# Keys and values of a head pair as two halves of 64 rows, products in two quadrants, zero products in waits, g_norm scaled late

## The chip, the cores and the metric

The kernel runs on one core of a Trainium2 chip. A core has five engines that run side by side and meet through semaphores: TensorE (matrix products; PE in the profile, with its weight loads as PEld), VectorE (DVE), ScalarE (ACT), GpSimd (POOL) and SyncE (SP), which here only issues DMAs. The metric is the device time of one launch in microseconds, the median of several runs; lower is better.

## The reference

Eight batches, eight heads, 576 tokens, head width 64. First a linear attention with a normalisation per head and token, then a block that mixes over tokens with waves of learned phases.

```python
kv  = einsum('bhsd,bhse->bhde', k, v)
out = einsum('bhsd,bhde->bhse', q, kv)
x   = out / sqrt(mean(out * out, -1) + 1e-6) * g_norm      # heads side by side: (8, 576, 512)
theta = x @ w_theta
y = w_tok_r @ (x * cos(theta)) + w_tok_i @ (x * sin(theta))
u = x + y
result = u + max(u @ w_ch, 0)                              # (8, 576, 512) float32
```

All inputs are float32; k^T v is computed in float32, the later products in float16 with float32 sums.

## The kernel before

**How the work is cut.** 576 tokens are four full tiles of 128 and a tail of 64 (`NF` = 4, `NT` = 5, `T` = 64). Heads are taken in pairs (`HP` = 4). For a batch:

- `load` (L274) issues the DMAs of q, k and v of a head pair. In batches 1 to 7 the tile is [128 rows, 2 heads, 4 tokens, 64], 256 KB in pieces of 1 KB, and the last 64 tokens of all heads come in extra loads `ql`, `kl`, `vl` (L301, 128 KB in pieces of 256 bytes); `kl` and `vl` land in the two constant buffers `tails`, whose rows 64 to 127 are zeroed once (L247). In batch 0 k and v come as [96 rows, 2 heads, 6 tokens, 64] (L282) and have no tails.
- `attention` (L483) forms k^T v of a head pair in float32 into PSUM: head 0 of the pair into partitions 0 to 63, head 1 into 64 to 127. That is ten products (five tiles by two heads, L498) in batches 1 to 7, twelve in batch 0 (six by two, L491), each in two records of the profile. `keep` (L510, L622) copies the result into a block diagonal float16 matrix `kvbd`, of which there are two, zeroed at the start.
- `cast_q`, `turn_q` turn q into float16 and transpose it (by DMA, L444, from batch 2 on; on TensorE in batches 0 and 1).
- `norm` (L524) for each tile: `raw` = q kv (L537), squares on ScalarE (L544), sums on VectorE (L548), the power -1/2 on GpSimd (L555, L559), x = raw times that (L571). Batch 0 has its own form in `first` (L593), by head pair, with roots on ScalarE.
- `turn_x` (L731): x transposed on TensorE and scaled by g_norm as it is copied out (L748; L680, L682 in batch 0). The scale `gcol` is loaded at the very start by two GpSimd DMAs (L943) and multiplied by 8 by a VectorE instruction (L376).
- `phase` (L760): theta (L770, L775), the whole turns taken off (L782, L786), sine and cosine (L805, L813), z = x times these (L823).
- `mix` (L845): eight results `y` of nine products each (L857) from z of all tiles and the transposed mixers `wT`; `uT` = y times gcol plus x^T (L865).
- `channel` (L878): u @ w_ch (L901), u transposed back (L892), the result (L912) and its store (L919, L924).

**Weights.** `load_weights` (L321) brings w_theta, the two token mixers and w_ch in chunks into staging buffers `wst` (four of them), and casts each on whichever of ScalarE, VectorE and GpSimd (L341, L343, L347) is chosen. `mixer_step` (L386) transposes the mixers on TensorE (L399) and copies them out (L407, L409).

**What sets the order.** Nothing runs as it is written down. Every piece is a task with its engines, planned costs, a due time, what it needs and which buffers it makes and uses. `Weave.run` (L74) walks through planned time: on each engine, among the tasks that could start within `SLACK` of the earliest, it takes the one with the earliest due time (`DUE`, by stage, batch and index), emits it, and notes planned ends. Loads keep one order of their own on SP; a load is put off while the planned DMA backlog is over `BACKLOG`. `in_traced_order` (L153) then pins each engine to the order in which the tasks were emitted. So each engine executes a fixed list, strictly in order, and waits where the plan was too hopeful. Planned costs never enter the program; they only shape these lists. How many buffers a kind of tile has is in `SLOTS`.

Of the kernel before, what the change touches and what calls it, by code (L numbers as in the profile page):

```python
# [21 lines left out]
    "load": (-17, 2.87),  # L22
    "first": (-0.52, 0.92),
    "cast": (-2.46, 2.3),
    "turn_q": (4.95, 0.2),
    "attention": (0.5, 3.82),
    "norm": (12.64, 4.8),
    "turn": (16.5, 4.83),
    "phase": (20.19, 4.95),
    "mix": (45.0, 2.9),  # L30
    "channel": (62.0, 4.75),
# [3 lines left out]
    "k": 5, "v": 5, "q": 6, "ql": 1, "tails": 2, "qc": 2, "qT": 2, "bd": 2, "sq": 2, "ss": 6,  # L35
    "rt": 6, "x": 9, "xT": 3, "pt": 2, "f": 2, "fa": 2, "tr": 2, "uT": 2, "u": 3, "ot": 3,
    "wst": 4, "z0": 2, "z1": 2, "z2": 2, "z3": 2, "z4": 2,
# [4 lines left out]
class Weave:  # L42
# [8 lines left out]
    SLACK = {"PE": 0, "ACT": 0.08, "DVE": 0.123, "POOL": 0.1, "SP": 0.05}  # L51
    MARGIN = {"PE": 0.014, "ACT": 0.018, "DVE": 0.106, "POOL": 0.1, "SP": 0.0}
    RATE = 0.335e6
    BACKLOG = 3.0
# [19 lines left out]
    def run(self):  # L74
        done, free, last = {}, {e: 0.0 for e in self.SLACK}, {}
# [22 lines left out]
        while ready:  # L98
            best = {}
            for t in ready:  # L100
                (name, engines, due, fn, needs, makes, uses, dma) = t
                if any(not self.slots[tag] for (tag, _) in makes):
                    continue
                at = max([done[n] for n in needs], default=0.0)
                for (tag, _) in makes:
                    at = max(at, min(self.slots[tag]))
                if dma is not None:
                    at = max(at, dma_free - self.BACKLOG)
                for (e, cost, lat) in engines:
                    start = max(free[e], at + self.MARGIN[e])  # L110
                    best.setdefault(e, []).append((start, due, at, t, cost, lat))
            picks = []
            for (e, c) in best.items():
                first = min(x[0] for x in c) + self.SLACK[e]
                (start, due, at, t, cost, lat) = min(
                    (x for x in c if x[0] <= first), key=lambda x: (x[1], x[0])
                )
                other = min(
                    (max(free[o], at) + k for (o, k, _) in t[1] if o != e), default=1e9
                )  # L120
                if other < max(free[e], at) + cost - 0.05:
                    start = max(start, other)
                picks.append((start, due, e, at, t, cost, lat))
            assert picks, [t[0] for t in ready][:40]
            (_, _, e, at, t, cost, lat) = min(picks, key=lambda x: x[:3])
            (name, engines, due, fn, needs, makes, uses, dma) = t
            start = max(free[e], at)
            free[e] = start + cost
            end = start + lat
            if dma is not None:  # L130
                (first, size, packed) = dma
                begin = max(start + first, dma_free)
                dma_free = begin + size / self.RATE / packed
                end = dma_free + 0.35
            done[name] = end
            for (tag, tile_name) in makes:
                pool = self.slots[tag]
                pool.remove(min(pool))
                last[tile_name] = 0.0
            fn(e)  # L140
            for tile_name in [n for (_, n) in makes] + list(uses):
                self.users[tile_name] -= 1
                last[tile_name] = max(last[tile_name], end)
                if self.users[tile_name] == 0:
                    self.slots[self.tag[tile_name]].append(last[tile_name] + 0.05)
            ready.remove(t)
            met(("t", name))
            for (_, tile_name) in makes:
                met(("b", tile_name))
        assert not wanted, list(wanted.items())[:5]  # L150
# [19 lines left out]
def kernel(  # L170
# [33 lines left out]
    NS = 6  # L204
    PS0 = S // NS
# [36 lines left out]
    tails = []  # L242
    for i in range(2):
        kl = const.tile([P, H, D], FP32, tag=f"kl{i}", name=f"kl{i}")
        vl = const.tile([P, H, D], FP32, tag=f"vl{i}", name=f"vl{i}")
        for t in (kl, vl):
            nc.gpsimd.memset(t[T:P], 0.0)  # L247
        tails.append((kl, vl))
# [21 lines left out]
    def dma(size, packed=1.0, first=1.4):  # L270
        return (first, size, packed)


    def load(b, hp):  # L274
# [3 lines left out]
        def part(kind, src):  # L278
            def fn(e):
                if b == 0 and kind != "q":  # L280
                    t = sb(kind, [PS0, 2, NS, D], FP32, f"{kind}{b}_{hp}")
                    nc.sync.dma_start(  # L282
                        out=t[:].rearrange("p h j d -> p h (j d)"),
                        in_=src[b, pair].rearrange("h (p j) d -> p h (j d)", j=NS),
                    )
                else:
# [4 lines left out]
                    )  # L291
                st[kind, b, hp] = t
            return fn

        def tail(kind, src):
            def fn(e):
                if kind == "ql":
                    t = sb("ql", [T, H, D], FP32, f"ql{b}")
                else:
                    t = tails[b % 2][0 if kind == "kl" else 1]  # L300
                nc.sync.dma_start(  # L301
                    out=t[0:T], in_=src[b, :, SF:S, :].rearrange("h s d -> s h d")
                )
                st[kind, b] = t
            return fn

        for (i, (kind, src)) in enumerate((("q", q), ("k", k), ("v", v))):
            weave.add((kind, b, hp), [SP], due("load", b, hp) + 0.01 * i, part(kind, src),
                      makes=[(kind, f"{kind}{b}_{hp}")], dma=dma(whole, 0.95), load=True)
        if hp == (0 if b else HP - 1):  # L310
            for (i, (kind, src)) in enumerate((("kl", k), ("vl", v), ("ql", q))):
                if b == 0 and kind != "ql":
                    continue
                weave.add((kind, b), [SP], due("load", b, hp) + (0.04 if b else -0.04) + 0.01 * i,
                          tail(kind, src),
                          makes=[("ql", f"ql{b}")] if kind == "ql" else
                          [("tails", f"tails{b}")] if kind == "kl" else [],
                          uses=[f"tails{b}"] if kind == "vl" else [],
                          dma=dma(whole / 2, 0.5), load=True)

    def load_weights():  # L321
# [13 lines left out]
        def cast(name, of, out, src, at, scale=1.0):  # L335
# [15 lines left out]
            weave.add(name, on, at, fn, needs=[of], uses=[of])  # L351

        at = due("load", 0, HP - 1) + 1.0
        for kc in range(NK):
            chunk(("wst", kc), moe_w_theta[kc * P:(kc + 1) * P, :], at + 0.01 * kc)
            cast(("wth", kc), ("wst", kc), wth[:, kc, :],
                 lambda kc=kc: st["wst", kc][:, 0:C], due("phase", 0, 0) - 1.0, FOLD)
        use = due("mix", 0, 0) - 8.0
# [10 lines left out]
        for kc in range(NK):  # L369
# [3 lines left out]
                 lambda kc=kc: st["wcs", kc][:, 0:C], due("channel", 0, 0) - 5.0)  # L373
# [5 lines left out]
        weave.add("gcol", [dve(0.1)], due("turn", 0, 0) - 2.0, gain)  # L379
# [3 lines left out]
        weave.add("sin", [("ACT", 1.5, 1.6)], due("phase", 0, 0), table,  # L383
                  needs=[("rt0", hp) for hp in range(HP + 1)])

    def mixer_step(n):  # L386
# [24 lines left out]
        at = due("mix", 0, 0) - 6.0 + 0.1 * n  # L411
# [71 lines left out]
    def attention(b, hp):  # L483
        def fn(e):
# [3 lines left out]
            if b == 0:  # L488
                for j in range(NS):
                    for r in range(2):  # L490
                        nc.tensor.matmul(  # L491
                            kvp[r * D:(r + 1) * D, hp, :], st["k", 0, hp][:, r, j, :],
                            st["v", 0, hp][:, r, j, :], start=(j == 0), stop=(j == NS - 1),
                        )
                return
            for j in range(NT):
                for r in range(2):
                    nc.tensor.matmul(  # L498
                        kvp[r * D:(r + 1) * D, hp, :],
                        st["k", b, hp][:, r, j, :] if j < NF else st["kl", b][:, 2 * hp + r, :],  # L500
                        st["v", b, hp][:, r, j, :] if j < NF else st["vl", b][:, 2 * hp + r, :],
                        start=(j == 0), stop=(j == NT - 1),
                    )

        def keep(e):
            for r in range(2):
# [4 lines left out]
                else:  # L511
                    nc.vector.tensor_copy(dst, src)

        weave.add(("kv", b, hp), [pe(0.84)], due("attention" if b else "first", b, hp), fn,
                  needs=[("k", b, hp), ("v", b, hp)] + ([("kl", b), ("vl", b)] if b else []),
                  makes=[] if hp else [("kv", f"kv{b}")],
                  uses=[f"k{b}_{hp}", f"v{b}_{hp}"] + ([f"tails{b}"] if b else [])
                  + ([f"kv{b}"] if hp else []))
# [419 lines left out]
    def due(stage, b, i):  # L938
        (first, every) = DUE[stage]
        return START + PERIOD * b + first + every * i  # L940

    for r in range(P // D):
        nc.gpsimd.dma_start(out=gcol[r * D:(r + 1) * D, :], in_=g_norm.unsqueeze(1))  # L943
    load_weights()
    for m in range(NM):
# [55 lines left out]
```

## Time and profile before

| | us |
|---|---|
| median of 5 runs | 244.79 (244.45 to 245.6) |
| the profiled execution | 243.88 |
| its span, first to last instruction | 242.1 |
| busy in the span: TensorE | 210.7 (87%), 2213 products |
| VectorE | 184.8 (76%) |
| ScalarE | 160.2 (66%) |
| GpSimd | 84.0 (35%) |
| DMA packets, share of 16 engines | 71.0% |
| products k^T v: L498 and L491 | 19.7 + 8.3 and 6.2 |

The span is what the trace covers; the time of a run is a little longer. Busy time of TensorE is the union of its records, whose ends are modelled, so a busy TensorE may still have room between its records; where times of single products are given below, they are distances from start to start. Rows of the profile name the line of the kernel, the engine, the tile written and the tiles read. A wait is put down to the instruction whose end released the waiting one.

### The profile page before, as it was taken

The page shows a single profiled execution, that of the slowest core. Times are in us where ns is not written, and L with a number is a line of the kernel's source. Part 1 is how long each engine was busy: PE and PEld are TensorE (multiplying, and loading weights), DVE is VectorE, ACT ScalarE, POOL GpSimd, SP SyncE. Part 2 cuts the span into 40 slices and gives each one's busy share as a digit, 9 for nine tenths or more (in the row PEclk, how much of TensorE's full clock was granted, in tenths as well). Part 3 has the DMA queues.
Part 4 walks back from the last instruction along what each step waited for, and adds up shares of the span by engine and source line. Part 5 has one row for each costly group of instructions (what it writes and reads, how often), then busy time and mean ns, then how long its engine had stood idle before and what let it go on. Part 6 is the DMA issues. An engine that isn't in the chain of part 4 may idle for free.

```text
span 242.1 us, 5707 instructions
## 1 busy us (share of the span) xinstructions
PE 210.7 (87%) x2213; PEld 144.7 (60%) x2213; DVE 184.8 (76%) x376; ACT 160.2 (66%) x303; POOL 84.0 (35%) x95
## 2 busy tenths in 40 slices
PE   0078586999997899989998999999999999999993
PEld 0066344777754675666665766766676766755861
DVE  1027669458996899789987997889879989998552
ACT  2036869763899288858884777677766797888021
POOL 7000034006550664076306640644136516640000
PEclk9999999599999999999999999999999999999999
DMA  6995589999946994995379986996499612002314
GB/s 186 219 204 152 154 273 232 329 355 232 341 94 165 316 250 95 274 368 126 77 188 265 331 100 172 279 317 170 100 259 337 94 63 109 26 22 87 111 43 152
DMA packets 60442, 46.41 MB, mean 192 GB/s; under 512 B 29056, under 2 KB 54144, under 8 KB 60416
## 3 DMA queue, kind: packets, MB, share of 16 engines
q1 hardware_dynamic: 60352, 46.05, 71.0%
q8 instruction: 17, 0.28, 0.5%
q14 instruction: 9, 0.07, 0.1%
q0 software_dynamic: 64, 0.00, 0.0%
HBM read 33.06 MB, written 9.44 MB: 176 GB/s over the span
## 4 chain that ended last, share of the span: by engine, by line
PE 32%; DVE 25%; POOL 21%; ACT 8%; DMA 8%; issue 4%; SPq 0%; DVEq 0%; POOLq 0%; ACTq 0%
POOL rt L559 16%; PE y L857 11%; DVE x L571 6%; DVE ss L548 5%; PE vps L901 4%; DMA gcol<-in_g_norm_dram 3%; PE kv L498 3%; POOL ss L555 3%; PE th L770 3%; DVE ot L912 3%; DVE f L786 3%; ACT tr L813 3%; DMA ql<-in_q_dram 3%; PE kv L491 2%; DVE z L823 2%
## 5 line engine op out<-in xcount | busy, mean ns | idle before, releaser
L857 PE MATMUL y<-wT,z 128*128 128x320 f16 (+1 forms) x576 | 79.1, 286 | 2.8 <-DVE z L823 1.4
L857 PEld LDWEIGHTS <-z 128*128 128x128 f16 x576 | 54.4, 98 | 19.5 <-issue 2.6
L559 POOL TENSOR_TENSOR rt<-ss,mhalf 128x8 f32<-128x8 f32 x35 | 61.8, 1765 | 2.9
L555 POOL TENSOR_SCALAR ss<-ss 128x8 f32<-128x8 f32 x35 | 11.9, 341 | 99.8 <-DVE ss L548 99.2
L748 ACT ACTIVATE xT<-xTps,gcol 128x512 f16<-128x512 f16 (+1 forms) x36 | 22.9, 637 | 22.2 <-PE xTps L739 22.2
L901 PE MATMUL vps<-wch,uT 128*128 128x512 f16 (+1 forms) x192 | 37.5, 344 | 0.0
L865 DVE SCALAR_TENSOR_TENSOR uT<-y,gcol,xT 128x256 f16<-128x256 f32 (+1 forms) x64 | 32.6, 511 | 6.4 <-PE y L857 6.2
L770 PE MATMUL th<-wth,xT 128*128 128x512 f16 x128 | 33.6, 390 | 0.2
L782 ACT ACTIVATE pt<-th,magic_t 128x512 f32<-128x512 f32 (+1 forms) x40 | 25.7, 642 | 11.8 <-PE th L770 9.2
L571 DVE TENSOR_TENSOR x<-raw,rt 128x512 f16<-128x512 f32 x36 | 24.8, 689 | 7.3 <-POOL rt L559 6.6
L908 ACT COPY u<-ups 128x512 f16<-128x512 f16 (+1 forms) x40 | 20.8, 538 | 12.6 <-PE ups L892 12.5
L912 DVE SCALAR_TENSOR_TENSOR ot<-vps,u 128x512 f32<-128x512 f32 (+1 forms) x40 | 25.0, 632 | 5.2 <-ACT u L908 3.2
L823 DVE TENSOR_TENSOR z<-x,tr 128x1024 f16<-128x1024 f16 (+1 forms) x40 | 25.7, 641 | 4.0 <-ACT tr L813 3.3
L548 DVE TENSOR_REDUCE ss<-sq 128x8 f32<-128x512 f32 x36 | 24.2, 679 | 2.7 <-ACT sq L544 2.5
L786 DVE SCALAR_TENSOR_TENSOR f<-pt,th 128x512 f32<-128x512 f32 (+1 forms) x40 | 25.1, 628 | 1.4 <-ACT pt L782 1.3
L805 ACT ACTIVATE tr<-f 128x512 f16<-128x512 f32 x32 | 20.2, 631 | 5.7 <-DVE f L786 5.3
L805 ACT ACTIVATE tr<-fa,pio_t 128x512 f16<-128x512 f32 x32 | 23.0, 718 | 1.0 <-DVE fa L793 1.0
L544 ACT ACTIVATE sq<-raw 128x512 f32<-128x512 f32 x36 | 20.9, 588 | 1.0 <-PE raw L537 0.9
L901 PEld LDWEIGHTS <-uT 128*128 128x128 f16 (+1 forms) x192 | 14.4, 102 | 9.2 <-issue 0.8
L498 PE MATMUL kv<-v,k 128*64 128x64 f32 x448 | 19.7, 234 | 0.0
L770 PEld LDWEIGHTS <-xT 128*128 128x128 f16 x128 | 11.9, 101 | 11.5 <-issue 1.5
L498 PEld LDWEIGHTS kv<-v,k 128*64 128x64 f32 x448 | 16.2, 143 | 4.2 <-issue 2.8
(83 smaller groups left out, 231.6 us busy)
## 6 DMA issues: line engine op xcount, KB each, us to landing
q<-in_q_dram SPq DMA_DIRECT2D x32, 256.0 KB, 5.7
out_dram<-ot SPq DMA_DIRECT2D x32, 256.0 KB, 5.0
k<-in_k_dram SPq DMA_DIRECT2D x28, 256.0 KB, 5.5
v<-in_v_dram SPq DMA_DIRECT2D x28, 256.0 KB, 5.7
k<-in_k_dram SPq DMA_DIRECT2D x4, 288.0 KB, 8.3
v<-in_v_dram SPq DMA_DIRECT2D x4, 288.0 KB, 9.4
wmix<-in_moe_w_tok_r_dram SPq DMA_DIRECT2D x4, 288.0 KB, 2.9
wmix<-in_moe_w_tok_i_dram SPq DMA_DIRECT2D x4, 288.0 KB, 3.5
```

The costliest lines, as they stand in the source:

```text
L498: nc.tensor.matmul(kvp[r * D:(r + 1) * D, hp, :], st["k", b, hp][:, r, j, :] if j < NF else st["kl", b][:, 2 * hp + r, :], st["v", b, hp][ ...
L548: nc.vector.reduce_sum(out=t[:], in_=st[sq][:].rearrange("p (h e) -> p h e", h=H), axis=mybir.AxisListType.X,)
L559: nc.gpsimd.tensor_tensor(out=r[:], in0=t[:], in1=mhalf[:], op=ALU.pow)
L571: nc.vector.tensor_tensor(out=t[:].rearrange("p (h e) -> p h e", h=H), in0=st[raw][:].rearrange("p (h e) -> p h e", h=H), in1=st[rt][:].un ...
L770: nc.tensor.matmul(t[:], xT[:, kc, :], wth[:, kc, :], start=(kc == 0), stop=(kc == NK - 1),)
L786: nc.vector.scalar_tensor_tensor(out=t[:], in0=st[pt][:], scalar=MAGIC, in1=st[th][:], op0=ALU.subtract, op1=ALU.subtract,)
L805: nc.scalar.activation(out=t[:, which, :], in_=src[:], func=AFT.Sin, scale=-RAD, bias=0.0 if bias is None else bias[:],)
L823: nc.vector.tensor_tensor(out=t[:], in0=xb.unsqueeze(1).broadcast_to((P, w, C)), in1=st[tr][:, 0:w, :], op=ALU.mult,)
L857: nc.tensor.matmul(t[:], z[:, kc * P:(kc + 1) * P], wT[m][:, cols], start=(m == 0), stop=(m == NM - 1),)
L865: nc.vector.scalar_tensor_tensor(out=st["uT", b][:, kc, cols], in0=st[y][:], scalar=gcol[:], in1=st["xT", b][:, kc, cols], op0=ALU.mult, o ...
L901: nc.tensor.matmul(t[half], uT(kc), wch[:, kc, r * n:(r + 1) * n], start=(kc == 0), stop=(kc == NK - 1),)
L912: nc.vector.scalar_tensor_tensor(out=t[:], in0=st[vp][:], scalar=0.0, in1=st[u][:], op0=ALU.max, op1=ALU.add,)
```

## The change

Several edits that go together:

1. k and v of a head pair become one tile [128 rows, 9 tokens, 64] in all batches: rows 0 to 63 hold the first head, rows 64 to 127 the second, each row nine consecutive tokens (2.3 KB). `kl`, `vl`, the `tails` buffers and their four memsets go; `ql` stays. k and v have six buffers each instead of five.
2. The products: nine token positions by two heads, each over 64 rows, head 0 from rows 0 to 63 into partitions 0 to 63, head 1 from rows 64 to 127 into partitions 64 to 127: two quadrants of the array. The planned cost goes from 0.84 to 0.6.
3. `idle_work`: up to 120 tasks, each one product of the zeros in `kvbd` into an `mm` bank, with no due time to speak of. They are taken where the plan finds nothing else for TensorE, up to planned time 40 (`WARM`). Nothing reads them.
4. g_norm is loaded by a task on GpSimd, and its scaling on VectorE needs that task (planned 9 us after its issue) instead of being free to go first.
5. Eight staging buffers instead of four. Mixers and w_ch are cast on GpSimd alone, w_theta on ScalarE or VectorE alone.
6. Planned start times of the engines (`BEGIN`), other due times (with own ones for parts of batch 0 and for the weights), slacks, margins, the backlog, and planned DMA sizes.

```diff
 DUE = {
-    "load": (-17, 2.87),
-    "first": (-0.52, 0.92),
-    "cast": (-2.46, 2.3),
-    "turn_q": (4.95, 0.2),
-    "attention": (0.5, 3.82),
+    "load": (-15.33, 2.93),
+    "theta": (17.06, 0.36),
+    "mixers": (20.83, 4.62),
+    "wch": (39.28, 1.45),
+    "wT": (24.0, 0.2),
+    ("phase", 0): (22.11, 0.97),
+    ("mix", 0): (30.68, 3.57),
+    ("channel", 0): (45.0, 5.48),
+    "first": (-2.84, 0.02),
+    "cast": (6.68, 2.3),
+    "turn_q": (4.23, 0.69),
+    "attention": (1.6, 3.82),
     "norm": (12.64, 4.8),
-    "turn": (16.5, 4.83),
-    "phase": (20.19, 4.95),
+    "turn": (15.31, 4.83),
+    "phase": (19.07, 4.95),
     "mix": (45.0, 2.9),
-    "channel": (62.0, 4.75),
+    "channel": (62.18, 4.5),
...
-    "k": 5, "v": 5, "q": 6, "ql": 1, "tails": 2, ...
+    "k": 6, "v": 6, "q": 6, "ql": 1, ...
-    "wst": 4, ...
+    "wst": 8, ...
...
-    SLACK = {"PE": 0, "ACT": 0.08, "DVE": 0.123, "POOL": 0.1, "SP": 0.05}
-    MARGIN = {"PE": 0.014, "ACT": 0.018, "DVE": 0.106, "POOL": 0.1, "SP": 0.0}
+    SLACK = {"PE": 0, "ACT": 0.052, "DVE": 0.064, "POOL": 0.1, "SP": 0.05}
+    MARGIN = {"PE": 0.011, "ACT": 0.06, "DVE": 0.119, "POOL": 0.1, "SP": 0.0}
     RATE = 0.335e6
-    BACKLOG = 3.0
+    BACKLOG = 3.5
+    BEGIN = {"PE": 1.6, "ACT": 2.2, "DVE": 1.7, "POOL": 2.5, "SP": 0.7}
+    WARM = 40.0
...
+                    if name[0] == "warm" and start > self.WARM:
+                        continue
...
-    NS = 6
-    PS0 = S // NS
+    PH = P // 2
+    NS = S // PH
...
-    tails = []
-    for i in range(2):
-        kl = const.tile([P, H, D], FP32, tag=f"kl{i}", name=f"kl{i}")
-        vl = const.tile([P, H, D], FP32, tag=f"vl{i}", name=f"vl{i}")
-        for t in (kl, vl):
-            nc.gpsimd.memset(t[T:P], 0.0)
-        tails.append((kl, vl))
...
+    def idle_work(n):
+        name = f"warm{n}"
+
+        def fn(e):
+            t = ps("mm", [P, C], FP32, name)
+            nc.tensor.matmul(
+                t[:], kv_bd[1][:, 0, :], kv_bd[1][:].rearrange("p h c -> p (h c)"),
+                start=True, stop=True,
+            )
+
+        weave.add(("warm", n), [("PE", 0.22, 0.25)], 1e6, fn, makes=[("mm", name)])
...
+                else:
+                    t = sb(kind, [P, NS, D], FP32, f"{kind}{b}_{hp}")
+                    nc.sync.dma_start(
+                        out=t[:].rearrange("p j d -> p (j d)"),
+                        in_=src[b, pair].rearrange("h (p j) d -> (h p) (j d)", j=NS),
+                    )
...
-            weave.add(name, on, at, fn, needs=[of], uses=[of])
+            weave.add(name, on[2:] if pool else on[:2], at, fn, needs=[of], uses=[of])
...
+        def fetch(e):
+            for r in range(P // D):
+                nc.gpsimd.dma_start(out=gcol[r * D:(r + 1) * D, :], in_=g_norm.unsqueeze(1))
...
-        weave.add("gcol", [dve(0.1)], due("turn", 0, 0) - 2.0, gain)
+        weave.add("gain", [("POOL", 1.3, 9.0)], -100.0, fetch)
+        weave.add("gcol", [dve(0.1)], due("first", 0, 1), gain, needs=["gain"])
...
-            if b == 0:
-                for j in range(NS):
-                    for r in range(2):
-                        nc.tensor.matmul(
-                            kvp[r * D:(r + 1) * D, hp, :], st["k", 0, hp][:, r, j, :],
-                            st["v", 0, hp][:, r, j, :], start=(j == 0), stop=(j == NS - 1),
-                        )
-                return
-            for j in range(NT):
+            for j in range(NS):
                 for r in range(2):
+                    half = slice(r * PH, (r + 1) * PH)
                     nc.tensor.matmul(
-                        kvp[r * D:(r + 1) * D, hp, :],
-                        st["k", b, hp][:, r, j, :] if j < NF else st["kl", b][:, 2 * hp + r, :],
-                        st["v", b, hp][:, r, j, :] if j < NF else st["vl", b][:, 2 * hp + r, :],
-                        start=(j == 0), stop=(j == NT - 1),
+                        kvp[r * D:(r + 1) * D, hp, :], st["k", b, hp][half, j, :],
+                        st["v", b, hp][half, j, :], start=(j == 0), stop=(j == NS - 1),
                     )
...
-        weave.add(("kv", b, hp), [pe(0.84)], due("attention" if b else "first", b, hp), fn,
+        weave.add(("kv", b, hp), [pe(0.6)], due("attention" if b else "first", b, hp), fn,
...
-    for r in range(P // D):
-        nc.gpsimd.dma_start(out=gcol[r * D:(r + 1) * D, :], in_=g_norm.unsqueeze(1))
     load_weights()
+    for n in range(120):
+        idle_work(n)
```

## The prediction

> **What bounds the kernel now.** I read the page's second part first (busy tenths in 40 slices of 6.05 us), then the chain of waits, the waits by pair, the DMA view in 3 us stretches, and last the sums over one long stretch.
>
> ```profile
> PE   0078586999997899989998999999999999999993
> DVE  1027669458996899789987997889879989998552
> DMA  6995589999946994995379986996499612002314
> ```
>
> There are two kernels in one. From about slice 8 on TensorE is at 9 nearly always: a long stretch that TensorE bounds. Ahead of it lie 50 us in which TensorE first does nothing (two slices), then works in scraps, while DMA is at 9, falls to 4 in slices 3 and 4, and rises again. The same stretch as a sum (columns: stretch, length, then busy time and instructions of PE, PEld, DVE, ACT, POOL, the clock, DMA share, GB/s):
>
> ```profile
> 51.00:237.00 186.00, 179.65 (x1892) 122.44 (x1889) 158.37 (x310) 130.97 (x244) 73.72 (x70) 1.00 0.67 183
> ```
>
> So the end is made up of 51 (until the first mixing product, L857, at 50.9) + 179.65 TensorE work + 6.35 idle + 5.1 tail (237 to 242.1). VectorE has 27.6 us free there, ScalarE 55, DMA a third. Whatever lengthens TensorE's work counts almost in full; whatever brings the 51 forward counts too.
>
> What holds the first 50 us, from the waits by pair (columns: us in all, times, longest):
>
> ```profile
> PE qTps0h L603 <- DVE qcast L420: 13.7, 1, 13.7
> DVE gcol L376 <- DMA gcol<-in_g_norm_dram: 11.7, 1, 11.7
> SPq L331 <- DMA wst<-in_moe_w_theta_dram: 5.1, 1, 5.1
> ```
>
> VectorE executes in order, and the first thing in its order is the scaling of g_norm (L376), whose DMA lands at 13.2; the first q had landed at 3.6 (issued 0.72, 2.9 to landing). The third line is the DMA queue itself: four staging buffers "wst" are full of w_theta, so the mixers' loads don't go out until a cast frees one (5.1 + 3.4 + 2.9 + 2.6 us of such waits in all, the cause of the two slack DMA slices).
>
> The price of the products k^T v, from the chain of waits (start, us, what):
>
> ```profile
> 14.34 1.48 PE kv L491 x24
> ...
> 32.31 1.72 PE th L770 x4
> ...
> 42.38 1.26 PE kv L498 x20
> ...
> 51.90 0.73 PE kv L498 x20
> ```
>
> Twenty records cost 1.26 us at 42 and 0.73 at 52, and four 512-column products 1.72 us at 32 against 0.86 later: the clock is at half until 34 and again from 41.6 to 48.3. (The page's clock row says 9 before that; single records contradict it.) And the DMA's pace, 6:9 us first, then 30:33:
>
> ```profile
> DMA packets 535, 0.68 MB, mean 226 GB/s; under 512 B 34, under 2 KB 535, under 8 KB 535
> q1 hardware_dynamic: 535, 0.68, 110.7%
> ```
>
> ```profile
> DMA packets 371, 0.76 MB, mean 252 GB/s; under 512 B 43, under 2 KB 43, under 8 KB 371
> q1 hardware_dynamic: 371, 0.76, 85.9%
> ```
>
> At 6:9 (q in rows of 1 KB, k and v of batch 0 in 1.5 KB rows on 96 partitions) a full DMA carries 226/1.107 = 204 GB/s; at 30:33 (mixers, rows of 2.3 KB) 252/0.859 = 293.
>
> **What the Trainium skill says.** "FP8 and Floating Point Precision", TensorE Precision Notes: a true fp32 product is four passes through the array. The trace agrees: each product is two records, and a record of 64 fp32 columns takes 222 ns warm, as one of 128 fp16 columns does (219). "TensorE: Matmul & The Clock Gate", Part 1: the clock is at half after some 3.4 us without work and full after as much dense work; here 12 us without work are followed by 430 ns per 512-column product, and 215 from 34.5 on. Same page, Part 3 (The mechanism): tiles of the array run side by side, and products start and end in program order. Here the two column halves already do: asked one by one, records of r=0 and r=1 start 6 ns apart and the next pair 58 ns later (107 at half clock). "DMA: Bandwidth & Descriptors", Specifications: below 512 B per transfer the line rate is lost. At 39:42, with 1,538 of 1,777 packets under 512 B, 129% share carried 210 GB/s.
>
> **The change, part by part.**
>
> *Products in quadrants.* Before, a head pair is 5 tiles x 2 heads = 10 products = 20 records = 10 pair steps: 10 x 58.3 = 0.58, plus 0.15 to get in and out = 0.73. After, 9 x 2 = 18 products = 36 records = 18 pair steps. No row of the trace shows 64-row fp32 quadrants. Upper bound: the step stays 58.3, since halves of the columns were concurrent already and the passes depend on the columns streamed, not on the rows: 18 x 58.3 + 0.15 = 1.20 us. Lower bound: a quadrant pair streams without sharing its rows and the step halves: 18 x 29.2 + 0.15 = 0.68 (fp16 steps of 109 ns for 256 columns and 215.5 for 512 give 0.416 a column and 2.5 fixed, so 29.2 for 64). I take 1.20, because the fp16 pairs at 37.7 (256 columns, 109 ns a pair) show that two streams over the same rows don't slow each other, so there is no sharing for quadrants to end. 28 head pairs x 0.47 = 13.1 us more TensorE work (lower bound: 1.4 less). Batch 0: 1.20 warm against 1.48 now.
>
> *k, v loads and tails.* 14 tail loads of 128 KB in 256-byte pieces go, with 0.65 us of SP issue each (9 us of SP time), and k, v become 288 KB in 2.3 KB rows. In the dense stretch that is near nothing for DMA (0.98 us each at 293 against 0.73 at 350 GB/s plus a share of the tails), but ql stands 1.3 us earlier in SP's queue: VectorE's 1.33 us wait for it at 129 goes. At the start 8 loads x 288 KB = 2.36 MB take 8.0 us instead of 11.5: minus 3.5.
>
> *g_norm late.* POOL loses four memsets (1.9 us) and issues g_norm at 2.3; it lands near 11. The scaling stands later in VectorE's order, so the first cast runs at about 4 instead of 13.3. Next late there is v of the first pair (now 7.0, then about 6.3).
>
> *Eight staging buffers; casts of mixers and w_ch on POOL alone.* w_theta lands near 19.5 instead of 23.1. The mixers follow without the stall: 2.65 MB at 293 = 9 us, landed at 28.5 instead of 38.5. POOL casts each chunk in 0.65 + 0.43 us: 10 x 1.08 = 10.8, kept up with by the DMA, done by 31. Uncovered, it would cost the distance to the next wait, z below. Four POOL casts of w_ch (0.68 each) can push a `rt` back by that once: under 1 us, hidden by six `ss` buffers.
>
> *Zeros in waits.* Up to 120 products of kvbd (zeros), 0.22 us warm, fill TensorE where the plan sees it idle before 40 us. They halve the early durations: of the chain from v of the last pair to the last x^T, 8 us remain (kv 1.2; L622, L629, L669, L680 with 0.43 + 0.35 + 0.35 + 0.69; L636 to L658 with 0.60 + 0.69 + 0.30 + 0.20 + 0.69; queueing 2.5), against 11.3 now (20.8 to 32.1). They also stand in TensorE's order: a real product behind one waits for it, and each needs an "mm" bank, behind whose reader (L782, L786) it can stall everything.
>
> *New due times, slacks and margins* reorder work within a batch. They can win at most the 6.35 us of idle, and may lose as much; beyond the idle time below I take nothing for them.
>
> *The sum.* v of the last pair lands at 17.2 (20.8 - 3.5); th can start near 25; VectorE needs 5 x (0.68 + 0.42 + 0.70) = 9 us for the five tiles to z, and 1 for the last ScalarE step: mixing can start at 35 instead of 51. By then TensorE has done what it had done at 51 less about 1.5 us (k, v of batch 1 arrive from 28.5 to 40). Remaining work: 179.65 + 1.5 + 13.1 - 0.9 (two batch 1 pairs already done) = 193.4. Idle: 6.35 falls to 3, since TensorE is later everywhere and ql's wait goes. 35 + 193.4 + 3 + 5.1 = 236.5, that is 5.6 less than the span of 242.1. The profiled execution took 243.88, 1.8 around the span; the median is 244.79, 0.9 above it. Forecast: 244.79 - 5.6 = 239.2.
>
> **The rivals.**
>
> *Steps halve.* If the 58 ns were two streams taking turns, products cost 0.68: 35 + 179.65 + 1.5 - 1.4 + 7 idle + 5.1 = 226.9, or 229.6 us. For it: 58.3 is just twice 29.2, which turns taken would give too. Against: the pairs start 6 ns apart, and fp16 pairs share rows free of charge.
>
> *Slower: the fillers' queue.* One mechanism: TensorE's order is fixed and has no gaps left before 40 us, so every overrun adds up: the first 8 zero products cold (+0.21 each, 1.7), products longer than laid out (6 x 0.5 = 3), data landing later than laid out and a zero product waiting for a bank (4). Mixing starts at 44, the 13.1 are paid: 44 + 193.4 + 4 + 5.1 = 246.5, or 249.2 us. It decides from a mixing start of 40.6 on. For it: the first zero products are surely cold; against: the waits it fills are longer than it.
>
> *The start is hidden.* Batch 1's loads end near 40 and hold the norm stage there, so an early mixing only leaves idle later: 6 us idle give 242.2 us. It is inside the first case's edge.
>
> **How the numbers follow.** First case, with the hidden start in it, 0.50 (own range 235 to 244.5); steps halve 0.26; fillers' queue 0.24. About 0.3% (0.7 us) is what a measurement tells from no change. Faster: 0.43 + 0.26 + 0.01 = 0.70; same: 0.05 + 0.03 = 0.08; slower: 0.02 + 0.20 = 0.22. The range reaches down to just past the second case and up to the lighter half of the third: 227 to 247.5.
>
> **What would show it.** A record group of 36 in `kv`: 1.2 us (pair step 58) or 0.7 (29). VectorE's first cast near 4 us; SP's waits for wst gone; mixers landed by 29; first y near 35; the TensorE sum from there to 237 some 13 us up. I am wrong if y starts after 40, if the step is 29, or if the idle time between grows instead of falling.

## The result, and the profile after

| | before | after |
|---|---|---|
| median, us | 244.49 (79 runs, 242.35 to 248.09) | 243.16 (44 runs, 242.27 to 243.87) |
| ratio | | 0.9955, 95% interval 0.9943 to 0.9968 |
| span of the profiled execution | 242.1 | 241.3 |

The change makes the kernel faster by 0.45%, 1.3 us where 5.6 had been forecast: little, but the whole interval lies below 1. Ratios leave out runs more than 1.5% above the fastest of the same kernel (two of four in e4, one of six in e11 below); medians are over all runs. The busy tenths of the changed kernel, from its page:

```profile
PE   7999999999987999999999999999999999999993
DVE  1268686388977889779897988997789868997652
DMA  6996999963479648854886469944993412102314
```

The empty start is gone, and TensorE is at 9 nearly everywhere. That row misleads: the page's list has 23.2 us of it as products `warm` (L284), the zeros, and 40.5 as k^T v (L499), 6.3 more than L498 and L491 had before. So the span is cut anew, as in the prediction, at the first mixing product. Before, then after (columns: stretch, length, TensorE busy and instructions, clock, DMA share, GB/s):

```profile
50.76:237.95 187.19, 180.83 (x1907) 1.00 0.67 183
```

```profile
43.36:237.24 193.88, 191.49 (x2318) 1.00 0.57 171
```

Each line is read as a sum: start + busy + idle (length less busy) + tail (span less the stretch's end).

| | mixing starts | busy | idle | tail | span |
|---|---|---|---|---|---|
| before | 50.76 | 180.83 | 6.36 | 4.17 | 242.12 |
| after | 43.36 | 191.49 | 2.39 | 4.06 | 241.30 |
| difference | -7.40 | +10.66 | -3.97 | -0.11 | -0.82 |
| forecast for after | 35 | 193.4 | 3 | 5.1 | 236.5 |
| forecast difference | -16 | +13.75 | -3.35 | 0 | -5.6 |

The prediction cut at 51 and 237, so its differences compare better than its terms. Idle time and tail hold. The work grows by 3.1 less than forecast. The start of mixing comes forward by 7.4 instead of 16; it is at 43.4 and not at 35, and that is what the forecast gain is lost to. The price of the products is what had been taken: from the chain of waits after (start, us, what),

```profile
42.24 1.19 PE kv L499 x36
```

36 records take 1.20 us where 20 took 0.73; within them, pairs start 58 ns apart, as before. Where the start went shows in the timeline of TensorE (start, us, engine, line, operation, tiles, shape, count):

```profile
25.51 1.89 PE L768 MATMUL th<-wth,xT 128*128 128x512 f16 x8
...
30.39 0.63 PE L773 MATMUL th<-wth,xT 128*64 128x256 f16 x8
30.95 1.25 PE L284 MATMUL warm<-kvbd 128*128 128x512 f16 x3
32.04 0.38 PE L407 MATMUL wTps<-ident,wnat 128*128 128x128 f16 x4
...
32.51 1.25 PE L284 MATMUL warm<-kvbd 128*128 128x512 f16 x3
33.60 0.38 PE L407 MATMUL wTps<-ident,wnat 128*128 128x128 f16 x4
...
34.07 0.39 PE L284 MATMUL warm<-kvbd 128*128 128x512 f16 x1
34.39 1.26 PE L499 MATMUL kv<-v,k 64*64 64x64 f32 x36
35.59 0.41 PE L407 MATMUL wTps<-ident,wnat 128*128 128x128 f16 x4
...
36.08 0.60 PE L284 MATMUL warm<-kvbd 128*128 128x512 f16 x2
36.52 0.39 PE L407 MATMUL wTps<-ident,wnat 128*128 128x128 f16 x4
...
36.99 0.82 PE L284 MATMUL warm<-kvbd 128*128 128x512 f16 x3
37.65 0.38 PE L407 MATMUL wTps<-ident,wnat 128*128 128x128 f16 x4
...
38.12 0.82 PE L284 MATMUL warm<-kvbd 128*128 128x512 f16 x3
38.78 0.52 PE L407 MATMUL wTps<-ident,wtt 128*128 128x128 f16 x5
39.23 1.26 PE L499 MATMUL kv<-v,k 64*64 64x64 f32 x36
40.42 1.25 PE L284 MATMUL warm<-kvbd 128*128 128x512 f16 x5
41.51 0.72 PE L469 MATMUL qTps<-ident,qcast 128*128 128x128 f16 x10
42.17 1.26 PE L499 MATMUL kv<-v,k 64*64 64x64 f32 x36
43.36 1.16 PE L855 MATMUL y<-wT,z 128*128 128x256 f16 x9
```

Theta starts at 25.5 (forecast 25). From then on TensorE has no gap worth the name until mixing: 20 zero products and three groups of long products k^T v stand between the transposes of the mixers. Counted from start to start, the 17.85 us are theta 4.0, transposes of the mixers 4.2, k^T v 3.6, transposes of q 0.7 and zeros 5.4. A row without gaps can't show whether the work in it was waiting for something, or is itself what the rest waits for. That took experiments.

### The profile page after: what moved, and what is told of

Its sections match the earlier page's. It is cut to its first block, busy times and chain, and to the rows that moved or that the text cites. A ratio compares the mean times of both kernels' runs of the same rounds, so it can differ in the third digit from the quotient of the medians.

```text
span 241.3 us, 6820 instructions
## 1 busy us (share of the span) xinstructions
PE 232.7 (96%) x2789; PEld 160.3 (66%) x2789; DVE 184.6 (77%) x369; ACT 158.8 (66%) x297; POOL 86.4 (36%) x104
## 4 chain that ended last, share of the span: by engine, by line
PE 90%; ACT 3%; DVE 2%; DMA 2%; issue 0%; SPq 0%; DVEq 0%
PE y L855 29%; PE kv L499 15%; PE vps L899 12%; PE th L768 11%; PE warm L284 7%; PE raw L535 4%; PE ups L890 4%; PE xTps L737 4%; DMA v<-in_v_dram 2%; PE th L773 2%; PE wTps L407 1%; ACT tr L811 1%; ACT tr L803 1%; PE qTps L469 0%; DVE f L784 0%
## 5 line engine op out<-in xcount | busy, mean ns | idle before, releaser
L855 PEld LDWEIGHTS <-z 128*128 128x128 f16 x576 | 53.7, 98 | 16.8 <-DVE z L821 2.0
L557 POOL TENSOR_TENSOR rt<-ss,mhalf 128x8 f32<-128x8 f32 x35 | 60.6, 1732 | 2.9
L553 POOL TENSOR_SCALAR ss<-ss 128x8 f32<-128x8 f32 x35 | 11.3, 322 | 95.5 <-DVE ss L546 94.9
L499 PEld LDWEIGHTS kv<-v,k 64*64 64x64 f32 x1152 | 36.1, 135 | 8.7 <-issue 6.7
L499 PE MATMUL kv<-v,k 64*64 64x64 f32 x1152 | 40.5, 221 | 0.4 <-DMA v<-in_v_dram 0.4
L780 ACT ACTIVATE pt<-th,magic_t 128x512 f32<-128x512 f32 (+1 forms) x40 | 25.7, 644 | 18.0 <-PE th L768 17.2
L768 PE MATMUL th<-wth,xT 128*128 128x512 f16 x128 | 32.8, 380 | 0.0
L284 PE MATMUL warm<-kvbd 128*128 128x512 f16 x80 | 23.2, 406 | 1.7 <-DVE pio_t L248 1.5
```

The source lines that it names most:

```text
L284: nc.tensor.matmul(t[:], kv_bd[1][:, 0, :], kv_bd[1][:].rearrange("p h c -> p (h c)"), start=True, stop=True,)
L499: nc.tensor.matmul(kvp[r * D:(r + 1) * D, hp, :], st["k", b, hp][half, j, :], st["v", b, hp][half, j, :], start=(j == 0), stop=(j == NS - 1),)
L557: nc.gpsimd.tensor_tensor(out=r[:], in0=t[:], in1=mhalf[:], op=ALU.pow)
L768: nc.tensor.matmul(t[:], xT[:, kc, :], wth[:, kc, :], start=(kc == 0), stop=(kc == NK - 1),)
L780: nc.scalar.activation(out=t[:], in_=st[th][:], func=AFT.Identity, bias=magic_t[:])
L855: nc.tensor.matmul(t[:], z[:, kc * P:(kc + 1) * P], wT[m][:, cols], start=(m == 0), stop=(m == NM - 1),)
```

## The experiments

All sums below are made like the one above, from the profiled execution; ratios are to the kernel before on the same chip.

**e1: what the products cost.** The first theory was that the longer products eat what the start wins.

```diff
-            for j in range(NS):
+            for j in range(NT):
...
-                        st["v", b, hp][half, j, :], start=(j == 0), stop=(j == NS - 1),
+                        st["v", b, hp][half, j, :], start=(j == 0), stop=(j == NT - 1),
```

> The changed kernel with the products k^T v over 5 of the 9 token positions only (it leaves the other 4 out of the sums); loads and every engine's order as in the changed kernel. 10 pair steps instead of 18, so 0.73 us a head pair instead of 1.20. If TensorE's longer products ate what the start won (theory A), its work from the first mixing product on falls by 13 us, some 4 us come back as idle time, and the time is 234 us (232 to 237). If the end is set by the normalisation chain or by loads and the longer products are mostly hidden (theory B), 240 us or more.

Measured: 229.55 us, ratio 0.941 (0.937 to 0.944), below even theory A's range. Sum: 40.34 + 181.46 + 3.11 + 4.06, of an execution 1.2 us slower than the median. The work falls by 10.0 and only 0.7 comes back as idle time, so the long stretch is TensorE's own; theory A holds. What neither theory had named is that mixing starts 3.0 earlier. Four pairs of batch 0 and three of batch 1 stand ahead of it, 7 x 0.47 = 3.3: nearly all of their length reaches the start. Theta starts at 23.89, 1.6 earlier, and the other 1.4, the whole of the three pairs of batch 1, falls between theta and mixing. TensorE's list is tight there.

**e2: the zeros taken out.**

```diff
         def fn(e):
-            t = ps("mm", [P, C], FP32, name)
-            nc.tensor.matmul(...)
+            return
```

> The changed kernel without the zero products; all other work in the same order on every engine. If the zeros stand in the way of the mixers' transposes and so are why mixing starts at 43.4 and not at 35 (theory Z), the first mixing product comes at 40 to 42 and the time falls to 240 to 242 us. If they pay by keeping the clock up and fill only waits that are there anyway (theory W), TensorE runs at half clock for most of the first 25 us, the first mixing product comes at 45 or later and the time is 244 to 247 us.

Measured: 240.15 us, ratio 0.982 (0.977 to 0.987); mixing starts at 42.19 in the profiled execution, the slowest of the six (241.94). Both theories are half right. The time falls, so the zeros cost more than they bring. But the clock does fall back without them. Theta in this run, from its timeline:

```profile
26.11 3.62 PE L764 MATMUL th<-wth,xT 128*128 128x512 f16 x8
```

Eight products take 3.62 us instead of 1.89. The zeros hold the clock and stand in the way at once.

**e6: zeros of half the length**, the run that parts the two.

```diff
-                t[:], kv_bd[1][:, 0, :], kv_bd[1][:].rearrange("p h c -> p (h c)"),
+                t[:, 0:C // 2], kv_bd[1][:, 0, :],
+                kv_bd[1][:, 0:2, :].rearrange("p h c -> p (h c)"),
```

> The changed kernel with zero products of 256 columns instead of 512, same order: 80 x 0.108 = 8.6 us less in TensorE's list, all of it before 42. If TensorE's list is what holds the first mixing product (theory L), it moves from 43.4 to 41 or earlier with the clock still up, and the time is 240 to 241.5 us. If the lists of ScalarE and VectorE hold it (theory S: the mixers' copies stand between the steps of the waves), it stays within 0.7 us and so does the time: 242.5 to 243.8.

Measured: 239.96 us, ratio 0.980 (0.975 to 0.984). The sum has one changed term: 40.12 + 191.49 + 2.40 + 4.08. Its timeline in the same place (in brackets, where TensorE was idle, for how long and what ended it):

```profile
23.51 1.89 PE L769 MATMUL th<-wth,xT 128*128 128x512 f16 x8
...
28.95 0.93 PE L284 MATMUL warm<-kvbd 128*128 128x256 f16 x3
29.72 0.38 PE L408 MATMUL wTps<-ident,wnat 128*128 128x128 f16 x4
...
32.13 1.26 PE L500 MATMUL kv<-v,k 64*64 64x64 f32 x36 [0.42 <-DMA v<-in_v_dram]
...
38.92 1.26 PE L500 MATMUL kv<-v,k 64*64 64x64 f32 x36
40.12 1.16 PE L856 MATMUL y<-wT,z 128*128 128x256 f16 x9
```

Theta still runs at full clock (1.89 for eight), 2.0 earlier, and mixing starts 3.24 earlier. Theory L holds: the zeros' length is paid at the start of mixing, though of the 8.6 us taken out of the list only 3.2 arrive there, 2.0 of them ahead of theta and 1.2 behind it. Part of the reason is the row at 32.13, the first k^T v of batch 1, which starts at 34.39 in the changed kernel: it stands in the list ahead of mixing and now waits for its v.

**e8: shorter copies of the mixers**, the test of theory S.

```diff
-                nc.scalar.copy(out=t[:], in_=st[name][:])
+                nc.scalar.copy(out=t[:, 0:64], in_=st[name][:, 0:64])
             else:
-                nc.vector.tensor_copy(t[:], st[name][:])
+                nc.vector.tensor_copy(t[:, 0:64], st[name][:, 0:64])
```

> The changed kernel with the nine copies of transposed mixers cut to 64 of 576 columns (it leaves out the rest of the mixers; zeros from a GpSimd memset stand there), order as in the changed kernel. Theory S (ScalarE's and VectorE's lists hold the start of mixing): 4.8 us of copies become 1.5 to 2, the first mixing product comes at 41 or earlier. Theory L (TensorE's list holds it): it stays within 0.7 us of 43.4.

Measured: one run, 243.52 us; mixing starts at 43.82, no earlier. ScalarE's timeline in this run:

```profile
34.68 0.21 ACT L418 COPY wT<-wTps 128x64 f16<-128x64 f16 x1 [0.90 <-PE wTps L410]
...
36.69 0.21 ACT L418 COPY wT<-wTps 128x64 f16<-128x64 f16 x1 [1.43 <-PE wTps L410]
```

The copies shrink to 0.21 us, and the time that they free turns into waits for TensorE's transposes. Theory S falls for zeros of full length; with shorter ones it wasn't tried.

**e9: zeros of a quarter of the length** (`t[:, 0:P]`, moving `kv_bd[1][:, 0, :]`).

> The changed kernel with zero products of 128 columns instead of 512, same order. If only TensorE's list still holds the start of mixing (theory L alone), another 4.3 us go from the list and mixing moves from 40.1 (zeros of 256) to 37 or earlier: 237 us. If by then loads, casts and the steps of the waves hold it, or if the thinner work lets the clock fall back, it stays within 1 us of 40 and the time at 239.3 to 241.

Measured: 239.26 us, ratio 0.982 (0.977 to 0.987); mixing starts at 39.74, within 0.4 of the half zeros, and the ratios of the two can't be told apart. The trace shows two of the rival's reasons, a load and the clock. The first k^T v of batch 1 starts at 32.20, again after a wait for v (0.45 us), so a shorter list ahead of it wins nothing more; from there to mixing 7.54 us pass, against 7.99 with half zeros and 8.97 in the changed kernel. And a record of k^T v at 11.1 takes 311 ns where it takes 218 later, so the thinner filling also warms TensorE later: theta starts at 23.93, 0.4 behind the half zeros.

**e5: the plan told the truth.**

```diff
-        weave.add(("kv", b, hp), [pe(0.6)], ...
+        weave.add(("kv", b, hp), [pe(1.15)], ...
```

> The changed kernel laid out with a planned cost of 1.15 for the products of a head pair instead of 0.6 (they take 1.20); nothing else changed, so that all lists are laid out anew. If the overrun of the plan is what puts the first mixing product at 43.4 instead of 35 (theory P), the layout takes fewer zero products ahead of it, mixing starts at 40 to 41 and the time is 240 to 241.5 us. If the overrun costs nothing in itself (rival), the start stays within 1 us and the time within 242.2 to 244.

Measured: 243.74 us, ratio 0.996 (0.993 to 0.998): the rival. Sum: 42.55 + 190.00 + 4.25 + 4.92. The layout takes 67 zero products instead of 80 and starts mixing 0.8 earlier, does 1.5 less work behind it, and gives both back as 1.9 us more idle time and 0.9 more tail. That the due times fitted the other plan may be why; it isn't shown.

**e3: g_norm scaled first again**, all else as changed.

```diff
+        for r in range(P // D):
+            nc.gpsimd.dma_start(out=gcol[r * D:(r + 1) * D, :], in_=g_norm.unsqueeze(1))
+        nc.vector.tensor_scalar(
+            out=gcol[:], in0=gcol[:], scalar1=math.sqrt(D), scalar2=None, op0=ALU.mult
+        )
...
         def fetch(e):
-            for r in range(P // D): ...
+            return
...
         def gain(e):
-            nc.vector.tensor_scalar(...)
+            return
```

> The changed kernel with g_norm's load and its scaling put first on GpSimd and VectorE again, all else in the same order. If the late scaling is worth what was counted, VectorE's first cast waits until about 11 instead of 5, theta starts 3 us later (28.5) and the time is 245 to 246.5 us. If the loads of the other head pairs hide it, theta stays within 1 us of 25.5 and the time within 0.3% of the changed kernel (242.5 to 243.9).

Measured: 248.84 us, ratio 1.018 (1.015 to 1.022). VectorE's timeline in this run:

```profile
8.82 0.15 DVE L380 TENSOR_SCALAR gcol<-gcol 128x1 f32<-128x1 f32 x1 [7.36 <-DMA gcol<-in_g_norm_dram]
8.90 0.75 DVE L431 CAST qcast<-q 128x512 f16<-128x512 f32 x2
```

The first cast moves from 3.45 to 8.90, theta from 25.5 to 30.2, mixing from 43.36 to 48.04, and nothing after it changes (191.49, 2.39, 4.06). That is more than forecast (theta at 28.5, 246.5 us at most). One small instruction at the head of a list carries 4.7 us to the end.

**e12: that part alone in the kernel before.**

```diff
         def gain(e):
-            nc.vector.tensor_scalar(...)
+            return
...
             if hp == 0:
                 st["xT", 0] = sb("xT", [P, NK, S], FP16, "xT0")
+                nc.vector.tensor_scalar(
+                    out=gcol[:], in0=gcol[:], scalar1=math.sqrt(D), scalar2=None, op0=ALU.mult
+                )
```

> The kernel before with one part of the change alone: g_norm's scaling on VectorE right ahead of the first copy that needs it, instead of first. VectorE's first cast runs at 4 instead of 13.3. If the late scaling is worth as much by itself as in the changed kernel (4.7 us of start), the time falls to 239 to 241 us. If the loads of mixers behind four staging buffers are the next wait in line (theory of waits in series), the first mixing product stays within 2 us of 50.8 and the time within 243 to 245.

Measured: 239.53 us, ratio 0.983 (0.977 to 0.988). My waits in series didn't happen: mixing starts at 47.15, 3.6 earlier, though four staging buffers and the half clock are still there. Its first cast, from the timeline:

```profile
3.65 0.83 DVE L418 CAST qcast<-q 128x512 f16<-128x512 f32 x1 [2.18 <-DMA q<-in_q_dram]
```

This one edit is worth more than the whole change. e3 is the other side of it: the change without this part takes 1.8% longer than the kernel before, so the other parts together lose. Which of them could be left as they were was tried for the products and the zeros only, not for the staging buffers, the casts and the due times.

**e4: 96 rows of six tokens in all batches**, 12 products.

```diff
-    PH = P // 2
+    PH = 96
...
-                    t = sb(kind, [P, NS, D], FP32, f"{kind}{b}_{hp}")
+                    t = sb(kind, [PH, 2, NS, D], FP32, f"{kind}{b}_{hp}")
...
-                        in_=src[b, pair].rearrange("h (p j) d -> (h p) (j d)", j=NS),
+                        in_=src[b, pair].rearrange("h (p j) d -> p h (j d)", j=NS),
```

> The changed kernel with k and v of all batches as 96 rows of 2 heads by 6 tokens (the form that batch 0 had before), 12 products in two column halves, no tails; every engine's order as in the changed kernel. If the price of a head pair goes by pair steps (theory A), 12 x 58.3 ns + 0.15 = 0.85 us instead of 1.20, 9.8 us less work for TensorE over 28 head pairs, of which 3 come back as idle time; the slower loads of the start (1.5 KB rows) cost 1 to 2: 238 us (235 to 241). If quadrants or the larger rows are what pays (rival), 243 us or more.

Measured: 243.01 us (239.38 to 244.19), ratio 0.986 (0.979 to 0.993), which rests on two runs: 239.38, in theory A's range, and 242.40, between the two forecasts. The price is as theory A has it, from this run's chain of waits:

```profile
96.74 0.85 PE kv L498 x24
```

But much of the saving doesn't arrive. The profiled execution was the longest of the four, so its sum shows the upper end: 45.66 + 183.80 + 8.88 + 4.08, so a start 2.3 later, 7.7 us less work and 6.5 more idle time. The same stretch of this run and of the changed kernel:

```profile
51.00:100.00 49.00, 40.61 (x478) 1.00 1.07 208
```

```profile
51.00:100.00 49.00, 46.66 (x633) 1.00 0.64 198
```

The DMA engines carry 208 GB/s at a share of 1.07 with 1.5 KB rows on 96 partitions, and 198 at 0.64 with 2.3 KB rows on 128. In this execution the loads become a bound: on its page 34% of the chain of waits is DMA, on the changed kernel's 2%. So the large rows of the change are likely worth something; whether by their size or by the 128 partitions wasn't tried.

**e7, e10, e11: products as before, start as after.** Batches 1 to 7 take k and v as 128 rows with tails again; batch 0 keeps the two halves. The tails are zeroed on GpSimd behind g_norm's load. e10 and e11 add the shorter zeros.

```diff
-                if kind == "q":
+                if kind == "q" or b:
                     t = sb(kind, [P, 2, NF, D], FP32, f"{kind}{b}_{hp}")
...
+            for j in range(NT if b else 0):
+                for r in range(2):
+                    (kt, vt) = (
+                        st[w, b, hp][:, r, j, :] if j < NF else st[f"{w}l", b][:, 2 * hp + r, :]
+                        for w in ("k", "v")
+                    )
+                    nc.tensor.matmul(
+                        kvp[r * D:(r + 1) * D, hp, :], kt, vt, start=(j == 0), stop=(j == NT - 1),
+                    )
```

> The changed kernel with k and v of batches 1 to 7 in their form before (128 rows, four tokens, tails with 256-byte pieces; tails zeroed on GpSimd after g_norm's load), batch 0 in two halves of 64 rows. 0.73 instead of 1.20 us for 28 head pairs: TensorE's busy time from the first mixing product on falls from 191.5 to about 181; idle rises from 2.4 to 5; mixing starts 1.4 earlier (three pairs stand before it). Theory A (start won, products paid back): 234 us (231 to 237). Rival (the small pieces of the tails and the extra loads hold the long stretch, as idle time): 239 or more.

> The form of k and v as before in batches 1 to 7 (as in the run with tails) and zero products of 256 columns. If the two effects are separate, the 3.2 us of the half zeros come on top of 238.9: 235.7 us (234.7 to 237). If an earlier start only turns into idle time later (loads of the long stretch decide), 238 to 239.

> As the run before, with zero products of 128 columns. The same question with the shorter list: 0 to 1.5 us below it if the clock stays up; above it by 1 us or more if the clock falls back to half in the first 40 us.

| | time | ratio (interval) | sum |
|---|---|---|---|
| e7 | 238.91 | 0.975 (0.971 to 0.979) | 43.05 + 182.57 + 7.70 + 4.16 |
| e10, zeros of 256 | 236.88 | 0.971 (0.966 to 0.976) | 39.07 + 182.53 + 7.70 + 4.17 |
| e11, zeros of 128 | 237.27 | 0.971 (0.965 to 0.978) | 40.76 + 182.62 + 7.69 + 4.17 |

e7 lies between its two forecasts. It has the 8.9 us less work, but idle time of 7.7 rather than the 5 expected, and a start that didn't move: the loads and the layout differ, and with them the list. The rival's reason isn't in the trace: 5.9 of the 7.7 us are waits of mixing for z, in four places, and the list of TensorE's waits names no load. e10 takes 4.0 off the start in its profiled execution and leaves the other terms alone; the medians, 2.0 apart, were taken on different chips, and the ratios, 0.4% apart, have intervals that overlap, so the size of that gain stays open. e10 and e11, which can't be told apart, are the fastest versions here that compute the whole result: 2.9% under the kernel before.

## Why the prediction was wrong

*Products in quadrants: right.* 18 pair steps of 58 ns and 1.20 us were taken, and measured. The rival in which the steps halve is out. The 13.1 us counted for 28 pairs are in the sum as +10.7 of work behind the start, and three of the pairs stand ahead of it; taking four of nine steps out in e1 gave 12.3 of span.

*Loads and theta: right in the number, in part by luck.* Theta came at 25.5 against 25, and the last mixer cast on GpSimd ends at 31.3 against 31. But v of the last pair of batch 0 was issued at 8.8 and took 6.4 to land: 15.2, not 17.2. From there to theta it took 10.3 us and not 7.8, and the two errors cancel. In e6, with half the zeros, v lands at 15.6 and theta follows 7.9 later, as forecast. So what the sum had left out already here is the zeros' length in TensorE's list.

*Idle time: right in size.* 2.4 against 3. *New due times:* taken at nothing, and no run tests them by themselves; in e5, a layout of its own under the same due times, idle time moves by 1.9 us.

*The sum's step from theta to mixing: wrong, and this is the step that failed.* I wrote that VectorE needs 9 us from theta to z and ScalarE 1 more, "mixing can start at 35 instead of 51". That is 10 us; the trace has 17.85. I had sized the stretch by VectorE's own work and let TensorE's list cost nothing. That list runs through it without a gap: 5.4 us of zeros and 12.5 of work that is needed, more than the 10 even with no zeros at all. With the two errors ahead of theta this gives the 8.4 by which mixing is late: 7.9 here, 2.5 from v to theta, less 2.0 for the earlier v.

What the runs show of it by experiment is less than the whole. The zeros' second half is worth 3.2 us of start, 2.0 of it ahead of theta (e6); the longer products 3.0, 1.6 of it ahead of theta (e1). The two don't simply add: e10 has half zeros and, in batch 1, the short products, and starts mixing only 1.1 earlier than e6, under a layout of its own. With shorter zeros the loads of batch 1 come next (the waits for v at 32 in e6 and e9). How early mixing could start with both out of the way, no run shows.

The mechanism was in the text, as the slower rival: a list without gaps, in which each overrun adds up. I gave it 0.24 and priced it at 9 us. It came with 8.4, and the 3 in it for longer products is what e1 measured. But 4 of its 9 were for data landing late and for zeros waiting for a bank, and v landed early, so that the totals agree so well is luck too. The work grew less than either case had it, and so the result lies between the two. The mistake was to treat as rivals what both hold at once. A filler that is harmless where its wait is real delays what stands behind it where the plan's wait is not.

*g_norm late:* the first cast at 3.45 was forecast as about 4. I didn't work out what the edit gives alone: 1.8% in the kernel before, with mixing 3.6 us earlier (e12), and 4.7 us of start in the changed one (e3).

## What to carry to other kernels

Look first at what stands at the head of each in-order list: one tiny instruction behind a slow DMA cost VectorE's first 10 us, and moving it alone gained 1.8%. A filler that keeps the clock up should be just long enough to do so; in a fixed list its length is paid wherever real work behind it is ready earlier than planned. When a step is sized by one engine's work, add up the lists of the others over the same step too. Cut the span at the point from which one engine bounds it, and write start + busy + idle + tail for each variant: a change that wins one term is easily seen to pay it back in another.

## What the runs showed of the hardware

- Float32 products over 64 rows in two quadrants run at the same pair step (58 ns) as over 128 or 96 rows in two column halves: 36 records of 64 rows take 1.20 us, 24 of 96 rows 0.85, 20 of 128 rows 0.73. Fewer rows buy nothing here; the number of products decides.
- In e6, zero products of 256 columns held the full clock as well as 512: the first k^T v, at 6.5, takes 1.26 us and theta 1.89. In e10, where a wait of 1.84 us stands before it, the first k^T v, at 7.45, still takes 1.85. With 128 columns k^T v was at half clock until past 11 us in e9 (records of 311 ns instead of 218) and until 9 in e11.
- The spread over runs: the kernel before 242.35 to 248.09 in 79 runs, the changed one 242.27 to 243.87 in 44, the half zeros 239.76 to 240.11 in four, without zeros 238.43 to 241.94 in six. It suggests that a held clock in the first 40 us makes a kernel scatter less, but e5 and e10 have the zeros too and spread over 2.5 us each (20 and six runs). What sets the spread isn't known.
